# Gated mix of attention and a gated MLP on one core: GpSimd's batches planned with the wait for the maxima and with what ran over, and the exchange of token mixtures issued from ScalarE's queue

## The chip, the core and the metric

The kernel runs on one core of a Trainium2 chip, as one launch. The metric is the device time of that launch in microseconds (us). The engines are PE (matrix multiplications, with the loading of weights shown apart as PEld), DVE (VectorE), ACT (ScalarE), POOL (GpSimd) and SP (SyncE, which only issues transfers here); each has a queue of its own and takes its instructions in order. Sixteen DMA engines carry what the queues issue.

## What is computed

For 2048 tokens x of width 512 the result mixes an attention with 32 heads of width 16 and a gated MLP of inner width 1792, all in float32:

```python
g = _sigmoid((x * gate_w).sum(-1, keepdims=True))
a = _A_ref(x, A_wqkv, A_wo)      # softmax(q k^T / 4) v for 32 heads, then @ wo
b = _B_ref(x, B_w_gate, B_w_up, B_w_down)   # (sigmoid(x @ w_gate) * (x @ w_up)) @ w_down
return g * a + (1 - g) * b
```

## The kernel before

**Precision.** Products of the dense parts are made of three terms: each operand is split into a high part and a low remainder (`xh`, `xl` for the tokens; `...h`, `...l` for weights), and high*high, high*low and low*high are summed.

**The attention, step by step.** Heads go in pairs, 16 pairs, and a pair takes 16 steps `k`, 256 steps in all. A step holds, for a pair that comes later, 8 score products only for their row maxima (PE L288, each reduced by DVE at L290); 8 score products whose exponential ACT takes (PE L675, ACT L677); and the 16 products with the values (PE L825), whose sum ACT copies out (L830) and POOL adds up (L842). The maxima of half a pair are complete in one step of eight. DVE then transposes them (`mt`, L296), and `put_max` has POOL split them into two parts (`mhl`, L315 and L306); SP writes these to memory and reads them back as two further rows of `qs` (L308, L312), so that the second score product comes out with its maximum subtracted.

**The dense sums beside it.** PE also works off twelve half products (L162) a step from a generator, `filling`: q and k of other head groups ("qk"), then for the MLP's gate and up weights (and the last of q and k) the jobs "far" (steps 16 to 47, counted from 0), "side" and "chain" (steps 48 to 71 for q and k, 72 to 239 for gate and up), and the first heads. A job's sum is quartered, so that most sums take one step. Its result stands in one bank of PSUM (`dn`); ACT copies it out at the start of the next step (`leave`, L603), POOL combines it with earlier results (`plus`, L536), and SP stores it. The two halves of the PE array write the same bank, so the second half of a sum may begin only when the first is through. `turn` orders this with an empty instruction on POOL's queue, a **token** (L173): it waits for PE's first half, and PE's second half (L162) waits for it. As POOL takes its queue in order, a token is also behind all that was put on POOL ahead of it.

**What sets POOL's order.** POOL's work lies in lists: `later` (sums and maxima), `turnover` (weights of the next job), `slow` (mixtures of tokens) and `soon`. Each entry has a cost in us. `work(2.0)` right behind the token in the middle of a step and `work(2.6)` at its end take entries off the lists while more than 0.3 us of that length is left; `put_max` is put ahead of the rest at a step's end.

**The exchange of mixtures.** The jobs "side" and "chain" do not read the tokens themselves but differences of quarters of them, which were made by POOL during "far" and stored in `t_d`. `mixed_x(n, c, k0, cx)` brings mixture n into a quarter of `xh` and of `xl`: two transfers of 512 KB (L372). It is called 14 times: twice when "far" ends, four times each in the last "side" job of q and k, in its last "chain" job, and in the last "side" job of gate and up. `kept_x` stores what is overwritten.

**Queues.** All transfers go out on SP's queue. ACT, PE, DVE and POOL keep the order in which the program is written; SP's order is chosen by the scheduler. Each transfer counts its end on one of eight counters (named DMAHW in the order shown below), which the transfers take in turn, and a transfer waits, where it is issued, until the one before it on its counter has ended. The weights of the next job are loaded by SP (L108) into two buffers that POOL has to have read (`ca`, `cb`: the parts of a "chain" weight).

Of the kernel before, what the change touches and what calls it, by code (L numbers as in the profile page):

```python
# [12 lines left out]
F32 = mybir.dt.float32  # L13
# [33 lines left out]
def gated_mix(ctx, tc, x, xT, wqk, wv, wo, w_gate, w_up, w_down, gate_w, out):  # L47
    nc = tc.nc
    pe, act, dve, pool, sp = nc.tensor, nc.scalar, nc.vector, nc.gpsimd, nc.sync
# [26 lines left out]
    t_d = dram.tile([5, 2, 2, 2, P, 512], F32, name="t_d")  # L76
# [100 lines left out]

    later, turnover, slow, soon = [], [], [], []

    def work(length):  # L180
        while length > 0.3 and (later or turnover or slow):
            cost, step = (later or turnover or slow).pop(0)
            step()
            length -= cost

    def flush(queue):
        while queue:
            queue.pop(0)[1]()
# [23 lines left out]
    def unit(w, c):  # L212
        cols = slice(c * 512, (c + 1) * 512)
        return [(w[k], (xh[:, k, cols], xl[:, k, cols])) for k in range(KT)]
# [17 lines left out]
    def put_qk(r, dst, row, c):  # L232
        e = keep.tile([P, 2, 512], F32R, name=f"qe{row}_{c}", tag="ev", bufs=2)
        split_later(e[:, 0, :], e[:, 1, :], r, lambda: sp.dma_start(
            dst[:, row * P:(row + 1) * P, c * 512:(c + 1) * 512].rearrange("a p s -> p a s"), e.bitcast(F32)))
# [63 lines left out]
    def put_max(half):  # L299

        p, i = half
        mt = mrow.pop(half)
        hl = keep.tile([P, 2, 32], F32R, name=f"mhl{p}_{i}", tag="mhl", bufs=2)

        def low():
            pool.tensor_tensor(hl[:, 1, :], mt, hl[:, 0, :].bitcast(F32), ALU.subtract)  # L306
            d = max_d[2 * p + i]
            sp.dma_start(d.rearrange("k r a j -> (k r) a j"), hl.bitcast(F32))  # L308
            for b in (1, 0):
                for a in range(2):  # L310
                    r = 64 * b + 3 * DH + a
                    rows_in[p, i] = sp.dma_start(QS[p % 2][r:r + 1, i * 1024:(i + 1) * 1024].rearrange(  # L312
                        "o (t k j) -> o t k j", t=8, k=4).bitcast(F32),
                        d[:, 8 * b:8 * b + 8, a, :].rearrange("k t j -> t k j").unsqueeze(0))
        return [(0.2, lambda: pool.tensor_copy(hl[:, 0, :], mt)), (0.25, low)]  # L315


    wd = []
# [1 line left out]
    def quarter(w, k0, c):  # L320

        cols = slice(c * 512, (c + 1) * 512)
        return [((w[0][:, k, :], w[1][:, k, :]), (xh[:, k0 + k, cols], xl[:, k0 + k, cols])) for k in range(2)]
# [44 lines left out]
    def mixed_x(n, c, k0, cx):  # L368

        cols = slice(cx * 512, (cx + 1) * 512)  # L370
        for a, xs in enumerate((xh, xl)):
            sp.dma_start(xs[:, k0:k0 + 2, cols].bitcast(F32), t_d[n, a, c].rearrange("k p s -> p k s"))  # L372

    def o_and_r(u, ks, ot, rb):

# [8 lines left out]
    def filling():  # L384
        pairs = [(m, i) for i in range(HF) for m in range(2)]
        qk = [(2, 0), (3, 0)]
# [6 lines left out]
        def beside(m, i):  # L393
            return i + HF if m < 2 else i + 1
# [68 lines left out]
        def out_of(run, name):  # L463
            e = keep.tile([P, 512], F32, name=name, tag="er", bufs=6)
            leave(e, run.o)
            return e
# [5 lines left out]
        def sums_of(kind, n, ws):  # L472

            if kind == "qk":
                for c in range(NC):
                    for i, w in enumerate(ws):
                        run = Sum(bankd(), unit(w, c))
                        yield run
                        put_qk(out_of(run, f"qk{n}_{c}_{i}"), (q_d, k_d)[i], n, c)
            elif kind == "far":  # L480
                for m in range(2):
                    for c in range(2):
                        run = Sum(bankd(), quarter(ws[m], 2, c))
                        yield run
                        sp.dma_start(place(m, n, c) if n < HF else place(2 + m, 0, c), out_of(run, f"far{m}{n}_{c}"))
            elif kind == "side":
                m, i = n
                for c in range(2):
                    for a in range(2):
                        run = Sum(bankd(), quarter(ws[a], 2 * a, c + 2))  # L490
                        yield run
                        if n in (qk[-1], pairs[-1]):
                            mixed_x(1 + a, c, 2 * a, c + 2)
                        e = out_of(run, f"side{m}{i}_{c}{a}")
                        if a == 0:
                            first = e
                            sp.dma_start(place(m, beside(m, i), c + 2), e)
                        else:
                            plus(e, e, first, place(m, i, c + 2))
            elif kind == "heads":  # L500
                for u in range(EARLY):
                    while split_of[u] in later:
                        later.pop(0)[1]()
                    oh, ol = [t for t in first_heads(u)][:2]
                    for a in range(2):
                        cols = slice(a * P, (a + 1) * P)
                        run = Sum(bankd(), [((oh[:, k, cols], ol[:, k, cols]), ws[k]) for k in range(2)])
                        yield run
                        sp.dma_start(hp_d[2 * u + a], out_of(run, f"hp{u}_{a}"))
            else:  # L510
                m, i = n
                for c in range(2):
                    i2 = beside(m, i)
                    to = [place(m, i, c), place(m, i, c + 2), place(m, i2, c + 2), place(m, i2, c)]
                    for a, (k0, cx) in enumerate(((0, c), (2, c), (0, c + 2), (2, c + 2))):
                        if a in (0, 2):
                            part = keep.tile([P, 2, 512], F32, name=f"had{m}{i}_{c}{a}", tag="ev", bufs=2)
                        had = part[:, a % 2]
                        if a < 3:
                            sp.dma_start(had, to[a])  # L520
                        run = Sum(bankd(), quarter(ws[a], k0, cx))
                        yield run
                        if n == qk[-1] and a >= 2:
                            mixed_x(1 + a, c, 2 * a - 4, c + 2)
                        e = out_of(run, f"chain{m}{i}_{c}{a}")
                        if a in (1, 2):
                            plus(e, e, first)
                        if a < 3:
                            plus(had, e, had, to[a])
                        else:  # L530
                            plus(e, e, first, to[a])
                        first = e
# [31 lines left out]
        for job, nxt in zip(jobs, jobs[1:]):  # L564
            kind, n = job
            coming = None
            for at, run in enumerate(sums_of(kind, n, ws)):
                if kind == "far":
                    u, r = divmod(4 * n + at - 2, 6)
                    if r == 0 and u < 4:  # L570
                        flush(slow)
                        mix_load(u // 2, u % 2)
                    if r == 2 and u < 4:
                        mix_x(u // 2, u % 2)
                if job == ("chain", pairs[-1]):
                    if at == 4:
                        for u in range(4):
                            first_heads_load(u)
                    if at in (6, 7):
                        first_heads_split(at - 6)  # L580
                if kind == "heads" and at in (2, 4, 6):
                    if at == 2:
                        first_heads_load(4)
                    first_heads_split(at // 2 + 1)
                if at == ask[kind][0]:
                    coming = raws(*nxt)
                if at == ask[kind][1]:
                    new = weights(*nxt, coming)
                    end = turnover[-1]
                yield run  # L590
            while end in turnover:
                turnover.pop(0)[1]()
            ws = new
            if kind == "far" and n == HF:
                flush(slow)
                for c in range(2):
                    mixed_x(0, c, 2, c)
                for c in range(2):
                    kept_x(3, c, 0, c + 2)
                    kept_x(4, c, 2, c + 2)  # L600
# [254 lines left out]
    run = next(fill)  # L855
# [29 lines left out]
    for k in range(NPER):  # L885
        n = 2 * k
# [17 lines left out]
        if run and run.done():  # L904
            run = next(fill, None)
# [99 lines left out]
    for n, (c, f) in enumerate(chunks):  # L1005
# [4 lines left out]
        hl = ready[n]  # L1010
# [59 lines left out]
```

## Time and profile before

| | |
|---|---|
| time, median of 3 runs | 1698.55 us (1698.15 to 1700.3) |
| profiled execution: its own time, its span, granted clock | 1699.21 us, 1697.4 us, 0.999 |
| busy DVE, ACT, POOL | 1453.4 us (86%), 1365.5 us (80%), 938.1 us (55%) |
| bytes moved | 254.20 MB, DMA engines busy 48.4% of the span |

A span goes from the first to the last instruction of the profiled execution. Rows of the timeline give start, duration, engine, line of the kernel, operation and tiles; in brackets the idle time just before, and what ended it. SPq and POOLq are entries of the queues of SP and POOL. A busy PE is not a PE without loss, since a product that is held up by the one ahead of it can show as a longer one.

### The profile page before, as it was taken

Reading aid. Unit: us, or ns where it says so; the run is one execution under the profiler, and the core shown is the slowest. Engines: PE = TensorE matmul, PEld = TensorE weight load, DVE = VectorE, ACT = ScalarE, POOL = GpSimd, SP = SyncE. Lnnn points to the kernel's source line nnn. Section 1 sums busy time; section 2 is a strip of 40 time slices with the busy share of each in tenths; the row PEclk is TensorE's granted clock in tenths of the full one; section 3 lists DMA queues with packets and bytes.
Section 4 is the critical chain, followed back from the end, with each engine's and each line's share of the span. In section 5 each row is a group of like instructions: output and inputs, shape, how many; then the busy total and the mean of one; then the engine's idle time right before and its main releaser. Section 6 shows DMA issues by size and latency. Waiting matters only on the chain.

```text
span 1697.4 us, 34663 instructions
## 1 busy us (share of the span) xinstructions
PE 1686.8 (99%) x12485; PEld 1030.4 (61%) x12485; DVE 1453.4 (86%) x2347; ACT 1365.5 (80%) x2657; POOL 938.1 (55%) x920
## 2 busy tenths in 40 slices
PE   9999999999999999999999999999999999999999
PEld 7755555555555565555555555555555555558887
DVE  7988888888889998898788888888998888888753
ACT  4188898888888898888889898898988989984331
POOL 1034575546665666566576676766666667544010
PEclk9999999999999999999999999999999999999999
DMA  7512456365465455455635352524343434358862
GB/s 243 141 48 58 128 198 181 132 182 184 138 205 150 149 148 175 141 166 159 176 101 144 107 144 97 141 97 139 105 134 108 127 119 156 123 180 288 295 212 72
DMA packets 143756, 254.20 MB, mean 150 GB/s; under 512 B 24224, under 2 KB 36512, under 8 KB 140704
## 3 DMA queue, kind: packets, MB, share of 16 engines
q1 hardware_dynamic: 143584, 251.98, 48.4%
q8 instruction: 98, 1.61, 0.4%
q14 instruction: 74, 0.61, 0.1%
HBM read 149.42 MB, written 102.50 MB: 148 GB/s over the span
## 4 chain that ended last, share of the span: by engine, by line
PE 97%; DMA 1%; POOL 1%; issue 1%; DVE 0%; ACT 0%; SPq 0%; POOLq 0%; DVEq 0%
PE dn L162 29%; PE sm L825 27%; PE sm L288 12%; PE st L675 7%; PE sm L1015 5%; PE sm L675 5%; PE st L288 3%; PE st L162 2%; PE dn L1015 2%; PE st L1015 2%; PE st L639 1%; PE st L149 1%; PE sm L149 1%; DMA chain_7r<-in_w_up_dram 1%; DMA chain_3r<-in_wqk_dram 0%
## 5 line engine op out<-in xcount | busy, mean ns | idle before, releaser
L290 DVE TENSOR_REDUCE stat<-sm 128x1 f32<-128x512 f32 x1313 | 850.8, 685 | 152.4 <-PE sm L675 132.1
L677 ACT ACTIVATE p<-st 128x512 f32<-128x512 f32 x1019 | 617.8, 652 | 1.2 <-PE st L675 0.8
L677 ACT ACTIVATE p<-sm 128x512 f32<-128x512 f32 x1027 | 610.4, 631 | 5.9 <-PE st L675 4.9
L288 PE MATMUL sm<-ks,qs 48*128 48x512 f32 x1313 | 515.8, 435 | 0.1
L290 DVE TENSOR_REDUCE stat<-st 128x1 f32<-128x512 f32 x735 | 480.9, 682 | 0.1
L825 PE MATMUL sm<-p,v 128*17 128x512 f32 x4016 | 480.8, 596 | 0.0
L675 PE MATMUL sm<-qs,ks 64*128 64x512 f32 x1027 | 428.8, 420 | 0.0
L675 PE MATMUL st<-qs,ks 64*128 64x512 f32 x1019 | 426.4, 419 | 0.2 <-ACT p L677 0.2
L288 PEld LDWEIGHTS sm<-ks,qs 48*128 48x128 f32 x1313 | 234.1, 184 | 287.6 <-DVE stat L290 206.8
L842 POOL TENSOR_TENSOR sum<-sum,part 128x512 f32<-128x512 f32 x224 | 288.6, 1288 | 147.1 <-PE sm L675 136.6
L288 PE MATMUL st<-ks,qs 48*128 48x512 f32 x735 | 290.2, 395 | 0.0
L830 ACT ACTIVATE part<-sm 128x512 f32<-128x512 f32 x214 | 128.4, 600 | 128.8 <-issue 94.1
L825 PEld LDWEIGHTS sm<-p,v 128*17 128x17 f32 x4016 | 93.3, 97 | 227.3 <-issue 158.0
L536 POOL TENSOR_TENSOR chain<-chain,chain 128x512 f32<-128x512 f32 x96 | 124.1, 1292 | 166.8 <-PE sm L675 148.6
L675 PEld LDWEIGHTS st<-qs,ks 64*128 64x128 f32 x1019 | 187.7, 184 | 30.6 <-issue 3.4
L675 PEld LDWEIGHTS sm<-qs,ks 64*128 64x128 f32 x1027 | 189.4, 185 | 10.8 <-issue 5.1
L536 POOL TENSOR_TENSOR had<-chain,had 128x512 f32<-128x512 f32 x96 | 123.5, 1287 | 29.8 <-PE sm L675 14.8
L288 PEld LDWEIGHTS st<-ks,qs 48*128 48x128 f32 x735 | 137.2, 187 | 1.5 <-ACT v L658 0.3
L603 ACT ACTIVATE chain<-dn 128x512 f32<-128x512 f32 x128 | 88.7, 693 | 0.0
L536 POOL TENSOR_TENSOR side<-side,side 128x512 f32<-128x512 f32 x32 | 41.3, 1292 | 84.8 <-PE sm L675 69.8
L104 POOL TENSOR_TENSOR ol<-ot,oh 128x512 fp32r<-128x512 f32 (+1 forms) x8 | 14.5, 1810 | 98.4 <-ACT oh L101 98.4
L315 POOL CAST mhl<-mt 128x32 fp32r<-128x32 f32 x32 | 7.6, 238 | 102.7 <-DVE mt L296 102.7
(913 smaller groups left out, 3230.6 us busy)
## 6 DMA issues: line engine op xcount, KB each, us to landing
gul<-gu_d SPq DMA_DIRECT2D x56, 512.0 KB
had<-gu_d SPq DMA_DIRECT2D x84, 256.0 KB
gu_d<-had SPq DMA_DIRECT2D x84, 256.0 KB
gu_d<-side SPq DMA_DIRECT2D x56, 256.0 KB
pv_d<-sum SPq DMA_DIRECT2D x32, 256.0 KB
qs<-q_d SPq DMA_DIRECT2D x30, 256.0 KB
ks<-k_d SPq DMA_DIRECT2D x30, 256.0 KB
gu_d<-far SPq DMA_DIRECT2D x28, 256.0 KB
```

Of the source, the lines that this page charges most:

```text
L149: pe.matmul(o, a, b, start=(i == 0), stop=(i == len(ops) - 1))
L162: mm = pe.matmul(self.o, a[rows], b[rows], start=(self.n == 0), stop=(self.n == 2 * len(self.ops) - 1))
L288: pe.matmul(t, qs[r:r + KM, qt * P:(qt + 1) * P], ks[r:r + KM, g * 512:(g + 1) * 512], start=True, stop=True)
L290: dve.tensor_reduce(stat[half][:, b, qt % 8, g:g + 1], t, axis=AX.X, op=ALU.max)
L536: pool.tensor_tensor(to, u, w, ALU.add)
L603: leave = lambda e, o: act.activation(e, o, AF.Copy)
L675: pe.matmul(o, ks[r:r + KR, (kt + a) * P:(kt + a + 1) * P], qs[r:r + KR, q0:q0 + 512], start=True, stop=True)
L677: act.activation(pt[:, 2 * a + c, :], o, AF.Exp, scale=DH ** -0.5)
L825: pe.matmul(o[32 * c:32 * c + VW, :], v[:, 2 * k % 16 + a, h * VW:(h + 1) * VW], pts[c // 2][:, 2 * a + c % 2, :], start=(a == 0), stop=(a ...
L830: act.activation(e, o, AF.Copy)
L842: pool.tensor_tensor(s, s, e, ALU.add)
L1015: pe.matmul(down[t], a, b, start=(f == 0 and m == 0), stop=(f == NF - 2 and m == 5))
```

## The change

`work` charges each call with what the call before ran over its length. The cost of `put_max`'s first entry goes from 0.2 to 1.6 us. `mixed_x` issues from ACT's queue, and its calls move behind the copy of the sum (`out_of`) that ends the step's reading; the two calls for mixture 0 move from the end of "far" into the first "side" job.

```diff
@@ -177,11 +177,15 @@
     later, turnover, slow, soon = [], [], [], []
 
+    over = [0.0]
+
     def work(length):
+        length -= over[0]
         while length > 0.3 and (later or turnover or slow):
             cost, step = (later or turnover or slow).pop(0)
             step()
             length -= cost
+        over[0] = max(0.0, -length)
@@ -312,7 +316,7 @@
-        return [(0.2, lambda: pool.tensor_copy(hl[:, 0, :], mt)), (0.25, low)]
+        return [(1.6, lambda: pool.tensor_copy(hl[:, 0, :], mt)), (0.25, low)]
@@ -369,7 +373,7 @@
         cols = slice(cx * 512, (cx + 1) * 512)
         for a, xs in enumerate((xh, xl)):
-            sp.dma_start(xs[:, k0:k0 + 2, cols].bitcast(F32), t_d[n, a, c].rearrange("k p s -> p k s"))
+            act.dma_start(xs[:, k0:k0 + 2, cols].bitcast(F32), t_d[n, a, c].rearrange("k p s -> p k s"))
@@ -489,9 +493,11 @@
                         run = Sum(bankd(), quarter(ws[a], 2 * a, c + 2))
                         yield run
+                        e = out_of(run, f"side{m}{i}_{c}{a}")
+                        if n == qk[0] and c == 1:
+                            mixed_x(0, a, 2, a)
                         if n in (qk[-1], pairs[-1]):
                             mixed_x(1 + a, c, 2 * a, c + 2)
-                        e = out_of(run, f"side{m}{i}_{c}{a}")
@@ -520,9 +526,9 @@
                         run = Sum(bankd(), quarter(ws[a], k0, cx))
                         yield run
+                        e = out_of(run, f"chain{m}{i}_{c}{a}")
                         if n == qk[-1] and a >= 2:
                             mixed_x(1 + a, c, 2 * a - 4, c + 2)
-                        e = out_of(run, f"chain{m}{i}_{c}{a}")
@@ -593,8 +599,6 @@
             if kind == "far" and n == HF:
                 flush(slow)
-                for c in range(2):
-                    mixed_x(0, c, 2, c)
                 for c in range(2):
                     kept_x(3, c, 0, c + 2)
                     kept_x(4, c, 2, c + 2)
```

Lines of the changed kernel are four higher behind `work`, more behind `sums_of`. The order of PE is the same in both, instruction for instruction, apart from line numbers. Three places where it moves:

POOL, in "far", at the end of a step that completes maxima (`mhl`) and the beginning of the next. `far02`, `far12` are weights of the next job, `mix` and `mh` mixtures, `sum` the sums of values. Before:

```order
L842 TENSOR_TENSOR sum_0_2094<-sum_0_2094,part_2289 128x512
L339 TENSOR_TENSOR mix_00_2146<-mix_00_2147,mix_00_2146 128x512
L315 CAST mhl_1_2350<-mt_1_2337 128x32
L306 TENSOR_TENSOR mhl_1_2350<-mt_1_2337,mhl_1_2350 128x32
L139 CAST far02h<-far02r 128x256
L136 TENSOR_TENSOR far02l<-far02r,far02h 128x256
L139 CAST far12h<-far12r 128x256
L136 TENSOR_TENSOR far12l<-far12r,far12h 128x256
L842 TENSOR_TENSOR sum_0_2094<-sum_0_2094,part_2370 128x512
```

and now:

```order
L846 TENSOR_TENSOR sum_0_2094<-sum_0_2094,part_2289 128x512
L319 CAST mhl_1_2349<-mt_1_2336 128x32
L310 TENSOR_TENSOR mhl_1_2349<-mt_1_2336,mhl_1_2349 128x32
L139 CAST far02h<-far02r 128x256
L136 TENSOR_TENSOR far02l<-far02r,far02h 128x256
L846 TENSOR_TENSOR sum_0_2094<-sum_0_2094,part_2367 128x512
L139 CAST far12h<-far12r 128x256
L136 TENSOR_TENSOR far12l<-far12r,far12h 128x256
L343 TENSOR_TENSOR mix_00_2146<-mix_00_2147,mix_00_2146 128x512
L343 TENSOR_TENSOR mix_00_2147<-mix_00_2147,mix_00_2146 128x512
```

A `mix` operation ahead of the maxima and the pair of `far12` behind them go behind the next sum, that is behind the token of the next step's middle.

SP, where the last "side" job of q and k ends and the first "chain" job begins. `chain_2r`, `chain_3r` are raw weights of the second "chain" job, `side_..` results. Before:

```order
L538 DMA s_d<-side_01_4663 128x512
L372 DMA xh<-t_d 128x2x512
L372 DMA xl<-t_d 128x2x512
L497 DMA s_d<-side_10_4730 128x512
L372 DMA xh<-t_d 128x2x512
L372 DMA xl<-t_d 128x2x512
L108 DMA chain_2r<-in_wqk_dram 128x2x256
L108 DMA chain_3r<-in_wqk_dram 128x2x256
L538 DMA s_d<-side_11_4793 128x512
```

and now:

```order
L544 DMA s_d<-side_01_4658 128x512
L108 DMA chain_2r<-in_wqk_dram 128x2x256
L503 DMA s_d<-side_10_4725 128x512
L108 DMA chain_3r<-in_wqk_dram 128x2x256
L544 DMA s_d<-side_11_4791 128x512
```

The four transfers of mixtures are gone from this stretch, and `chain_2r` stands ahead of the store of `side_10`.

ACT, the last of the 14 calls, with what each row waits for in brackets (PE, DVE, Pool, Activation: counters of the engines):

```order
L681 ACTIVATE p_1_9730<-st_65 128x512 [waits PE_49]
L607 ACTIVATE side_11_9751<-dn 128x512 [waits DMAHW0_49,PE_49]
L376 DMA xh<-t_d 128x2x512 [waits DMAHW6_49]
L376 DMA xl<-t_d 128x2x512 [waits DMAHW7_49]
L834 ACTIVATE part_9769<-sm_69 128x512 [waits DVE_49,PE_49,Pool_49]
L681 ACTIVATE p_0_9781<-sm_71 128x512 [waits PE_49,Activation_49]
```

The two transfers stand between the copy of the dense sum and the copy of the values' sum, and each waits for a counter of the transfers.

## The prediction

> **What bounds the kernel now.** First the page: what is busy, and the chain that ended last.
>
> ```profile
> PE 1686.8 (99%) x12485; PEld 1030.4 (61%) x12485; DVE 1453.4 (86%) x2347; ACT 1365.5 (80%) x2657; POOL 938.1 (55%) x920
> PE 97%; DMA 1%; POOL 1%; issue 1%; DVE 0%; ACT 0%; SPq 0%; POOLq 0%; DVEq 0%
> ```
>
> PE bounds it; PE's order stays as it is, so the change can win only what PE loses between its products. To see that loss I read a table by stretches for the products with the values alone (L825, 16 in a step), so that the count gives the steps.
>
> ```profile
> core 0: us, PE busy (x) PEld busy (x), PEclk, DMA share, GB/s
> 90.47:405.37 314.90, 107.06 (x896) 20.73 (x896) 1.00 0.45 140
> 405.37:412.52 7.15, 1.92 (x17) 0.38 (x18) 1.00 0.53 196
> 412.52:812.08 399.56, 135.71 (x1136) 26.24 (x1136) 1.00 0.54 161
> 812.08:827.47 15.39, 4.57 (x32) 0.81 (x32) 0.89 0.82 192
> 827.47:995.04 167.57, 57.34 (x480) 11.09 (x480) 1.00 0.39 117
> 995.04:1173.72 178.68, 61.24 (x516) 11.91 (x520) 1.00 0.40 120
> ```
>
> The last stretch is 32 steps (516 counts four of the next): 178.68/32 = 5.584 us a step, the undisturbed pace. Against it the others have lost: 56 steps 314.90 - 312.70 = 2.2; one step (the 57th) 7.15 - 5.58 = 1.6; 71 steps 399.56 - 396.46 = 3.1; two steps 15.39 - 11.17 = 4.2; 30 steps 0.05. Together 11.1 us, and no more can be won in these steps. Next, PEld's waits in the windows 90 to 450, 450 to 812 and 812 to 1460, of each the row on the token:
>
> ```profile
> PEld dn L162 <- POOLq L173: 3.6, 5, 1.5
> ...
> PEld dn L162 <- POOLq L173: 1.4, 4, 0.5
> ...
> PEld dn L162 <- POOLq L173: 2.6, 1, 2.6
> ```
>
> The 3.6 us answer to the first two losses (3.8). Of the 3.1 the token explains 1.4; the rest is not at a token and stays. The 2.6 us wait lies in the two steps that lose 4.2; there the granted clock is 0.89 over the stretch, and the rest of the loss goes with that clock.
>
> **The plan of POOL.** The timeline of POOL at one of these losses, with PEld's row at its end:
>
> ```profile
> 204.76 0.21 POOL L315 CAST mhl<-mt 128x32 fp32r<-128x32 f32 x1 [1.81 <-DVE mt L296]
> 205.05 0.25 POOL L306 TENSOR_TENSOR mhl<-mt,mhl 128x32 fp32r<-128x32 f32 x1
> 205.25 0.40 POOL L139 CAST far02h<-far02r 128x256 fp32r<-128x256 f32 x1
> 205.72 0.73 POOL L136 TENSOR_TENSOR far02l<-far02r,far02h 128x256 fp32r<-128x256 f32 x1
> 206.40 0.40 POOL L139 CAST far12h<-far12r 128x256 fp32r<-128x256 f32 x1
> 206.88 0.74 POOL L136 TENSOR_TENSOR far12l<-far12r,far12h 128x256 fp32r<-128x256 f32 x1
> ...
> 206.91 0.18 PEld L162 LDWEIGHTS dn<-xh,far01h 64*128 64x128 f32 x1 [0.69 <-POOLq L173]
> ```
>
> POOL stands 1.81 us for the maxima, which the plan had at nothing, then does four operations; the token is through when the last of them has begun (206.88), and PE goes on at 206.91, 0.69 late. With 1.6 us charged, the new order puts only `far02` ahead of the token: it is through at 205.72, and PE, which wanted it at 206.91 - 0.69 = 206.22, does not wait. The margin is 0.5 us. The other places of this kind have the same two small operations last or fewer. The two operations that go behind the token take 0.48 + 0.70 us there; with the sum and the two mixtures that the new order puts beside them (three of the size of L842, 1.28 us below) the batch is 5.0 us, under the 5.58 of a step. So the token waits away from weights go to nothing: 3.6 - 1.5 = 2.1 in the first stretch, 1.4 in the second. What they cost if a later batch then runs over: the same again, so the bounds are 0 and 3.5; I take **3.5**.
>
> **The exchange off SP's queue.** At the 57th step the token is behind weights that have not landed. SP's queue, POOL and PEld there:
>
> ```profile
> 395.70 0.48 SPq L497 DMA_DIRECT2D s_d<-side  x1
> 399.92 0.36 SPq L372 DMA_DIRECT2D xh<-t_d  x1
> 400.33 0.46 SPq L372 DMA_DIRECT2D xl<-t_d  x1
> 400.85 0.46 SPq L108 DMA_DIRECT2D chain_2r<-in_wqk_dram  x1
> 401.36 1.52 SPq L108 DMA_DIRECT2D chain_3r<-in_wqk_dram  x1
> ...
> 392.78 1.30 POOL L536 TENSOR_TENSOR side<-side,side 128x512 f32<-128x512 f32 x1
> ...
> 405.03 1.29 POOL L842 TENSOR_TENSOR sum<-sum,part 128x512 f32<-128x512 f32 x1
> 409.28 0.73 POOL L444 TENSOR_TENSOR chain_2r<-chain_2r,chain_3r 128x256 f32<-128x256 f32 x1 [2.96 <-DMA chain_3r<-in_wqk_dram]
> ...
> 410.93 0.18 PEld L162 LDWEIGHTS dn<-xh,cb(2, 0)h 64*128 64x128 f32 x1 [1.53 <-POOLq L173]
> ```
>
> From 396.2 to 399.9 SP stands at a mixture that waits for PE, and the weights behind it go out 4 us after they could. Now the mixtures are gone from SP. But the new plan of POOL also puts `side` and a `sum` ahead of the last two operations on the buffer that `chain_3r` goes into: these ended when `side` began, 392.78, and now end at 392.78 + 2 x 1.25 + 0.69 + 1.29 = 397.3 (spacing of rows: `side` and `sum` 1.25; cast 0.69). `chain_3r` can go out at 397.3 in place of 401.36, 4.1 earlier, with the last mixture behind it rather than ahead. If it takes as long as now (401.36 to 409.28), it lands at 405.2, and POOL is free at 405.03 + 1.25 = 406.3: no wait, with 1.1 us in hand. The token follows the first L444 by 410.93 - 409.28 = 1.65, so at 407.95, and PE wants it at 410.93 - 1.53 = 409.4. Won: **1.5**. The same 400 us later:
>
> ```profile
> 806.64 0.36 SPq L372 DMA_DIRECT2D xh<-t_d  x1
> 807.63 0.51 SPq L108 DMA_DIRECT2D chain_0r<-in_w_up_dram  x1
> 808.19 0.44 SPq L108 DMA_DIRECT2D chain_7r<-in_w_up_dram  x1
> ...
> 799.51 1.29 POOL L536 TENSOR_TENSOR side<-side,side 128x512 f32<-128x512 f32 x1
> ...
> 812.03 1.28 POOL L842 TENSOR_TENSOR sum<-sum,part 128x512 f32<-128x512 f32 x1
> 817.11 0.72 POOL L444 TENSOR_TENSOR chain_0r<-chain_0r,chain_7r 128x256 f32<-128x256 f32 x1 [3.80 <-DMA chain_7r<-in_w_up_dram]
> ...
> 818.75 0.18 PEld L162 LDWEIGHTS dn<-xh,cb(0, 0)h 64*128 64x128 f32 x1 [2.63 <-POOLq L173]
> ```
>
> `chain_7r` can go out at 799.51 + 4.5 = 804.0 instead of 808.19, and lands 4.2 earlier, at 812.9; POOL is free at 813.3. That margin is only 0.4 us, but the token, 1.64 later at 814.9, has 1.2 more before PE wants it at 818.75 - 2.63 = 816.1. Won: the whole **4.2**, the clock's part with it. Bounds for both places: 0 (nothing lands sooner) and 5.8; I take 5.7.
>
> **What ACT pays.** ACT's rows around the last of the 14 places, and the rows of L372 taken together (min/median/max ns):
>
> ```profile
> 807.28 0.70 ACT L603 ACTIVATE side<-dn 128x512 f32<-128x512 f32 x1
> 808.54 0.60 ACT L830 ACTIVATE part<-sm 128x512 f32<-128x512 f32 x1 [0.57 <-issue]
> ...
> L372 SPq DMA_DIRECT2D xh<-t_d x14: 360/410/535, 350.9 to 806.6; - x14
> L372 SPq DMA_DIRECT2D xl<-t_d x14: 378/482/1104, 351.4 to 807.1; - x14
> ```
>
> A pair costs SP 0.41 + 0.48 = 0.89 us; on ACT no issue is on show. If the queue issues while L603 runs, 1.26 us (808.54 - 807.28) cover it and it costs nothing; if it waits for L603's end, 0.57 cover it and 0.32 are left, 14 times 4.5 us, since behind L830 ACT's exponentials follow without idle time. That SP's rows follow one another while their data are still under way speaks for the first; I take **0** and keep 4.5 for the range. No new wait for PE comes in: the copy ahead of the transfers has waited for the same sum. What is queued behind is L830 and eight exponentials a step, and PE waits for these.
>
> **Sum.** 3.5 + 1.5 + 4.2 = 9.2 us. The profiled execution took 1699.21; less 9.2 is 1690.0. It lies 0.66 above the median of the runs, 1698.55, so a median would be 1689.4. I say **1689.7 us**, 0.5% faster.
>
> **The rivals.** (1) *ACT pays*: 4.5 us of the gain go back, 1694.2. For it: ACT's exponentials have no idle time. Against: the copy of the values' sum has to wait anyway. (2) *The transfers bound the two places*: the DMA share is 0.82 in the stretch from 812, the bytes are the same, and 5.7 us stay: 1695.4. Against: at 395.7 to 399.9 no weight was even put out. The Trainium skill, page "DMA: Bandwidth & Descriptors", section "Issuing engines are not separate DMA queues", says that transfers from all queues run on the same 16 engines and that a second queue saves only the time of issuing; taken alone that is this rival and its 1695.4. The trace differs at this place, where what is saved is a wait of SP's queue and not its issuing. (3) *The plan only shifts POOL's lateness* to later tokens, 938.1 us of work being the same: 3.5 less, 1693.2. (4) *Slower: ACT stands at a counter.* Each transfer now waits on ACT until the transfer before it on its counter has landed; that can be a weight put out a few us before. `chain_7r` took 817.11 - 808.19 = 8.9 us. At four of the 14 places (the second and fifth call, and the last two) that neighbour was put out within the step before; were it put out 5 us earlier and took 8.9, ACT would stand 3.9, less 0.57 of idle 3.3. Four times that is 13 us, against 9.2 won: 1702.9. It decides from 9.2/4 + 0.57 = 2.9 us a place on. Against: the weights among these neighbours go out sooner than before, as worked out above.
>
> **Chances.** Forecast 0.56, rivals (1) 0.14, (2) 0.11, (3) 0.09, (4) 0.10. A measurement can tell about 0.2%, 3.4 us, from no change. Against the execution's 1699.2 the forecast gains 9.2, (3) 6.0, (1) 5.0 and (2) 3.8, which is only just over it: all of the first two, most of (1) and half of (2) make faster 0.80; the rest of these and a weak (4) make same 0.11; slower is 0.09. The lower end is all 11.1 us won, 1699.21 - 11.1 - 0.66 = 1687.4; the upper end takes in (1) to (3) with some to spare, 1697.0. What is left out is mostly (4).
>
> **What would show it.** Right: no PEld row on POOLq at L173 over 0.3 us between 90 and 1460; the step at 57 and the two from 129 at 5.6 us and the granted clock 1.00 there; SP's `chain_3r` and `chain_7r` out some 4 us earlier against the step; POOL without a wait at L444. ACT's rows of the transfers (L376) start within 0.3 us of the copy ahead of them, and L834 still 1.26 us behind it. Wrong: L834 later than that by 0.3 (1) or by several us behind a transfer (4); L444 still waiting (2); new rows on POOLq in the step behind the maxima (3).

## The result, and the profile after

| | before | changed |
|---|---|---|
| median | 1698.35 us (1697.88 to 1700.3, 4 runs) | 1689.48 us (1688.66 to 1691.14, 4 runs) |
| ratio, 95% interval | | 0.9947, 0.993 to 0.9964 |
| profiled execution: time, span | 1699.21, 1697.4 us | 1689.49, 1687.7 us |

The forecast was 1689.7 us; the changed kernel is 0.5% faster. On the page, the busy times and the head of the chain that ended last:

```profile
PE 1680.0 (100%) x12485; PEld 1026.4 (61%) x12485; DVE 1452.3 (86%) x2347; ACT 1362.8 (81%) x2657; POOL 936.6 (55%) x920
PE 97%; issue 1%; DVE 1%; POOL 0%; DMA 0%; ACT 0%; SPq 0%; POOLq 0%; DVEq 0%
```

DVE, ACT and POOL have the work that they had. PE's time is shorter because products that were held up were counted as long ones: in steps 129 and 130 some 90 products kept PE busy for 13.19 us before, and for 11.17 us now. The table by stretches of the prediction, for the products with the values (now L829) of the changed kernel, cut at the same steps:

```profile
core 0: us, PE busy (x) PEld busy (x), PEclk, DMA share, GB/s
90.60:403.20 312.60, 107.05 (x896) 20.72 (x896) 1.00 0.47 143
403.20:408.79 5.59, 1.91 (x16) 0.37 (x16) 1.00 0.38 145
408.79:806.45 397.66, 135.71 (x1136) 26.22 (x1136) 1.00 0.55 162
806.45:817.62 11.17, 3.82 (x32) 0.74 (x32) 1.00 0.98 212
817.62:985.07 167.45, 57.34 (x480) 11.07 (x480) 1.00 0.39 120
```

Row by row against before: 314.90 - 312.60 = 2.30; 7.15 - 5.59 = 1.56; 399.56 - 397.66 = 1.90; 15.39 - 11.17 = 4.22; 167.57 - 167.45 = 0.12. Together 10.1 us. The two executions differ by 9.7; the 0.4 between is in the stretches ahead of the first step and behind these. The two steps from 129 now run at 5.58 us with the clock at 1.00, while the transfers are busy for 0.98 of that time.

PEld's waits over the whole span of the changed kernel, the row on the token ahead of the second halves of the dense sums (9.7 us, 14 times, before):

```profile
PEld dn L162 <- POOLq L173: 2.2, 4, 0.6
```

All four lie ahead of 90 us, in the opening; between 90 and 1460 us the view has no row on POOLq any more.

**The plan.** POOL's timeline at the place of the prediction (204.76 to 206.91 before), and PEld's row of the same step:

```profile
204.84 0.21 POOL L319 CAST mhl<-mt 128x32 fp32r<-128x32 f32 x1 [3.03 <-DVE mt L300]
205.13 0.25 POOL L310 TENSOR_TENSOR mhl<-mt,mhl 128x32 fp32r<-128x32 f32 x1
205.33 0.40 POOL L139 CAST far02h<-far02r 128x256 fp32r<-128x256 f32 x1
205.80 0.73 POOL L136 TENSOR_TENSOR far02l<-far02r,far02h 128x256 fp32r<-128x256 f32 x1
206.50 1.28 POOL L846 TENSOR_TENSOR sum<-sum,part 128x512 f32<-128x512 f32 x1
...
206.04 0.18 PEld L162 LDWEIGHTS dn<-xh,far01h 64*128 64x128 f32 x1
```

POOL now stands longer for the maxima, 3.03 us against 1.81, because less was put ahead of them. It costs nothing: the token is through at 205.80, and PE's second half starts at 206.04 with no bracket behind it.

**The exchange.** At the 57th step (from 403.2), SP, POOL and PEld of the changed kernel:

```profile
392.16 0.39 SPq L108 DMA_DIRECT2D chain_2r<-in_wqk_dram  x1
...
394.90 0.38 SPq L108 DMA_DIRECT2D chain_3r<-in_wqk_dram  x1
...
404.10 0.74 POOL L448 TENSOR_TENSOR chain_2r<-chain_2r,chain_3r 128x256 f32<-128x256 f32 x1
...
407.05 0.18 PEld L162 LDWEIGHTS dn<-xh,cb(2, 0)h 64*128 64x128 f32 x1
...
795.32 0.43 SPq L108 DMA_DIRECT2D chain_0r<-in_w_up_dram  x1
...
798.11 0.64 SPq L108 DMA_DIRECT2D chain_7r<-in_w_up_dram  x1
...
807.36 0.74 POOL L448 TENSOR_TENSOR chain_0r<-chain_0r,chain_7r 128x256 f32<-128x256 f32 x1
```

`chain_3r` goes out 8.3 us ahead of the step's start (403.20 - 394.90), where it was 4.0 (405.37 - 401.36); `chain_7r` 8.3 (806.45 - 798.11), where it was 3.9 (812.08 - 808.19). L448, which had stood 2.96 and 3.80 us for them, has no wait.

**ACT.** Its timeline at one of the 14 places of the changed kernel (ACTq is its queue):

```profile
392.24 0.41 ACTq L376 DMA_DIRECT2D xh<-t_d  x1
392.31 0.69 ACT L681 ACTIVATE p<-st 128x512 f32<-128x512 f32 x1
392.69 0.51 ACTq L376 DMA_DIRECT2D xl<-t_d  x1
392.79 0.70 ACT L607 ACTIVATE side<-dn 128x512 f32<-128x512 f32 x1
394.08 0.60 ACT L834 ACTIVATE part<-sm 128x512 f32<-128x512 f32 x1 [0.59 <-PE sm L829]
```

Both transfers go out before the copy L607, which stands ahead of them in the program, has begun; the first even before the exponential ahead of that. L834 follows the copy after 1.29 us, as before, and waits for PE only.

### The profile page after: what moved, and what is told of

Its sections match the earlier page's. It is cut to its first block, busy times and chain, and to the rows that moved or that the text cites. A ratio compares the mean times of both kernels' runs of the same rounds, so it can differ in the third digit from the quotient of the medians.

```text
span 1687.7 us, 34644 instructions
## 1 busy us (share of the span) xinstructions
PE 1680.0 (100%) x12485; PEld 1026.4 (61%) x12485; DVE 1452.3 (86%) x2347; ACT 1362.8 (81%) x2657; POOL 936.6 (55%) x920
## 4 chain that ended last, share of the span: by engine, by line
PE 97%; issue 1%; DVE 1%; POOL 0%; DMA 0%; ACT 0%; SPq 0%; POOLq 0%; DVEq 0%
PE dn L162 30%; PE sm L829 27%; PE sm L292 13%; PE st L679 7%; PE sm L1019 5%; PE sm L679 4%; PE st L292 2%; PE dn L1019 2%; PE st L162 2%; PE st L1019 2%; PE st L643 1%; PE st L149 1%; PE sm L149 1%; PE st L829 0%; DVE stat L294 0%
## 5 line engine op out<-in xcount | busy, mean ns | idle before, releaser
L829 PE MATMUL sm<-p,v 128*17 128x512 f32 x4016 | 480.0, 595 | 0.0
L829 PEld LDWEIGHTS sm<-p,v 128*17 128x17 f32 x4016 | 93.1, 96 | 225.9 <-issue 155.1
L834 ACT ACTIVATE part<-sm 128x512 f32<-128x512 f32 x214 | 128.1, 599 | 126.5 <-issue 86.0
L607 ACT ACTIVATE chain<-dn 128x512 f32<-128x512 f32 x128 | 89.1, 696 | 0.0
```

The source lines that it names most:

```text
L607: leave = lambda e, o: act.activation(e, o, AF.Copy)
L829: pe.matmul(o[32 * c:32 * c + VW, :], v[:, 2 * k % 16 + a, h * VW:(h + 1) * VW], pts[c // 2][:, 2 * a + c % 2, :], start=(a == 0), stop=(a ...
L834: act.activation(e, o, AF.Copy)
```

## The experiments

Each kernel was timed against the kernel before on the same chip. Where steps are named, a step's length is the time from its first product with the values to that of the next step, read from the rows of that line; an undisturbed one is 5.58 us. The text counts steps from 1, as the prediction does; some expectations below count them from 0 (their 196 is the 197th).

| kernel | median (range), us | ratio to before, 95% interval |
|---|---|---|
| plan_only | 1696.04 (1691.18 to 1698.65) | 0.9978, 0.9968 to 0.9989 |
| exchange_only | 1693.89 (1692.93 to 1695.83) | 0.9971, 0.9958 to 0.9983 |
| on_sp | 1694.46 (1692.14 to 1696.62) | 0.9973, 0.9961 to 0.9985 |
| act_ahead | 1696.04 (1693.59 to 1697.87) | 0.9988, 0.9978 to 0.9997 |
| cost_only | 1689.42 (1689.03 to 1690.25) | 0.9945, 0.9932 to 0.9957 |
| carry_only | 1691.08 (1690.45 to 1691.3) | 0.9953, 0.9941 to 0.9966 |
| four_issues | 1705.32 (1703.32 to 1706.18) | 1.0036, 1.0024 to 1.0049 |
| dve_spread | 1691.04 (1690.52 to 1693.07) | 0.9955, 0.9942 to 0.9969 |
| first_early | 1691.39 (1691.1 to 1693.84) | 0.9957, 0.9944 to 0.9971 |
| dens_only | 1688.08 (1687.4 to 1690.07) | 0.9937, 0.9924 to 0.9949 |
| after_again | 1689.61 (1688.78 to 1689.72) | 0.9943, 0.993 to 0.9957 |
| cost_dens | 1689.16 (1688.07 to 1689.61) | 0.9941, 0.9929 to 0.9953 |

### One half of the change alone

plan_only is the kernel before with the two lines of the plan:

```diff
+    over = [0.0]
+        length -= over[0]
+        over[0] = max(0.0, -length)
-        return [(0.2, lambda: pool.tensor_copy(hl[:, 0, :], mt)), (0.25, low)]
+        return [(1.6, lambda: pool.tensor_copy(hl[:, 0, :], mt)), (0.25, low)]
```

> Only the plan of POOL (1.6 us for the maxima, and the charge for what ran over); the exchange stays on SP's queue at its old places. If the two parts add up, as the prediction has it, the token waits behind the maxima go (3.5 us) and those at the 57th and the 129th step stay (about 5.7 us of loss): 1694.9 us. If the plan only shifts POOL's lateness, or the later release of the weights' buffer delays the weights further, those two waits grow and the time is 1697 us or more. If the plan alone ends the two waits too, 1689 to 1690.

exchange_only is the kernel before with `mixed_x` on ACT's queue and its calls where the change has them:

```diff
-            sp.dma_start(xs[:, k0:k0 + 2, cols].bitcast(F32), t_d[n, a, c].rearrange("k p s -> p k s"))
+            act.dma_start(xs[:, k0:k0 + 2, cols].bitcast(F32), t_d[n, a, c].rearrange("k p s -> p k s"))
```

> Only the exchange: issued from ACT behind the copies, mixture 0 in the first side job; POOL's plan as before. If the parts add up: the waits at the 57th and 129th step go (5.7 us), the token waits behind the maxima stay (3.5 us): 1692.7 us. If the exchange needs the new plan to win, over 1695.

What PEld still waits for at tokens between 90 and 1460 us, first in plan_only:

```profile
PEld dn L162 <- POOLq L173: 3.6, 2, 3.1
```

then in exchange_only:

```profile
PEld dn L162 <- POOLq L173: 3.8, 9, 0.7
```

The halves part cleanly. With the plan alone the waits behind the maxima are gone and the two places of the exchange are left (two waits, the longest 3.1 us); with the exchange alone these two are gone and nine short ones behind the maxima are left. The medians are 2.4 and 4.6 us under the kernel before of their call (1698.49), 7.0 together, against 8.9 for both: the halves do not add. By the steps, the losses up to the 244th fall by 3.6 and 5.1 us, and by 10.1 with both. Of the 1.4 between, 0.6 is in plan_only at the exchange, where steps 129 and 130 take 9.99 and 7.08 us, 1.7 more than before, and step 57 takes 1.1 less; the rest is spread in exchange_only over single steps that lose 0.1 to 0.3 us, and why these come is not settled.

The two places of plan_only can be followed further. The weights go out as far ahead of the step as before (3.84 us at the 129th step, 3.89 before; 3.96 and 4.01 at the 57th), so a later release of their buffer is not it. What differs is when POOL can use them: 9.35 us behind the issue of `chain_7r`, where it was 8.92, and 6.76 behind that of `chain_3r`, where it was 7.92. At the 129th step the wait at the token grows from 2.63 to 3.12 us, and over the two steps the granted clock is 0.80 where it was 0.89. The ten runs of plan_only spread from 1691.18 to 1698.65 us, with a mean granted clock of 1.000 in the shortest and 0.997 in the longest; what these two waits cost differs from run to run, and the profiled execution is one of the long ones. That can be one reason why the medians do not add.

### The new places, but SP's queue

```diff
-            act.dma_start(xs[:, k0:k0 + 2, cols].bitcast(F32), t_d[n, a, c].rearrange("k p s -> p k s"))
+            sp.dma_start(xs[:, k0:k0 + 2, cols].bitcast(F32), t_d[n, a, c].rearrange("k p s -> p k s"))
```

> The changed kernel, but the mixtures are issued from SP's queue at the new places in the program (behind the copies, mixture 0 in the first side job). If what is won is SP's queue no longer standing at a mixture that waits for PE, the two waits at weights come back and the time is about 1695 us. If the moved places alone do it, 1689.5 us as changed.

SP and POOL of this kernel at the 57th step:

```profile
397.81 0.36 SPq L376 DMA_DIRECT2D xh<-t_d  x1
398.22 0.53 SPq L376 DMA_DIRECT2D xl<-t_d  x1
398.80 0.82 SPq L108 DMA_DIRECT2D chain_2r<-in_wqk_dram  x1
399.72 0.42 SPq L108 DMA_DIRECT2D chain_3r<-in_wqk_dram  x1
...
407.56 0.72 POOL L448 TENSOR_TENSOR chain_2r<-chain_2r,chain_3r 128x256 f32<-128x256 f32 x1 [3.37 <-DMA chain_3r<-in_wqk_dram]
```

and PEld's waits at tokens, 90 to 1460 us:

```profile
PEld dn L162 <- POOLq L173: 4.6, 2, 2.6
```

The weights again go out behind the last mixture, 4.8 us later than in the changed kernel (399.72 against 394.90), and POOL stands for them. By the medians the kernel is 5.0 us slower than the changed one. The bytes, the plan and the places are the same: the gain at these two steps is SP's queue being free. This tells against rival (2), and so does the share of 0.98 at full pace in the changed kernel. The rule of the Trainium skill, page "DMA: Bandwidth & Descriptors", section "Issuing engines are not separate DMA queues", that a second queue saves only the time of issuing, does not cover these 5.0 us: they are waits of the queue.

### Mixtures ahead of the copy

```diff
-                        e = out_of(run, f"side{m}{i}_{c}{a}")
                         if n == qk[0] and c == 1:
                             mixed_x(0, a, 2, a)
                         if n in (qk[-1], pairs[-1]):
                             mixed_x(1 + a, c, 2 * a, c + 2)
+                        e = out_of(run, f"side{m}{i}_{c}{a}")
```

and the same in "chain".

> The changed kernel, but the mixtures stand ahead of the copy of the dense sum on ACT's queue instead of behind it. ACT then waits for PE's sum at the transfer. If issuing runs ahead of ACT's arithmetic, as the changed kernel's profile shows it (a transfer's row begins before the copy does), the time stays at 1689.5 us within 1 us. If the issue time of about 0.9 us counts in front of the copy, the bank of the dense sum comes free later and 14 places cost 0.3 us or more each: 1694 us or more.

Neither came. Almost the whole loss is one step, the 128th, of 13.03 us. ACT's timeline there, with SP's row of the transfer that it names:

```profile
799.59 0.61 SPq L251 DMA_DIRECT2D qs<-q_d  x1
...
802.09 0.37 ACTq L376 DMA_DIRECT2D xh<-t_d  x1
802.21 0.68 ACT L681 ACTIVATE p<-st 128x512 f32<-128x512 f32 x1
808.05 0.37 ACTq L376 DMA_DIRECT2D xl<-t_d  x1
808.46 0.60 ACT L607 ACTIVATE side<-dn 128x512 f32<-128x512 f32 x1 [5.57 <-DMA qs<-q_d]
```

The second transfer shares a counter with a load of `qs` that SP put out at 799.59. ACT's queue stands until that has landed: its transfer goes out 8.5 us behind the load's issue, and the copy and the exponentials behind it stand with it. This is rival (4), at one place and at 5.57 us. By the counters in the two traces it is met because swapping the calls also shifts which transfer shares which counter: in the changed kernel the neighbour of the second transfer is an `xh` of ACT's own, out at 795.49, and the pair goes out at 801.08 and 801.48 without a stand. The first transfer of the pair has `chain_0r` as its neighbour in both kernels, out 5.7 to 5.8 us ahead of it and landed in time. Of that place apart, three steps (67, 68 and 72) lose 1.2 us in sum, and the other places nothing; that fits the first theory of the issues themselves. What the 1.2 us are was not tested.

### Twice the issues

```diff
-            act.dma_start(xs[:, k0:k0 + 2, cols].bitcast(F32), t_d[n, a, c].rearrange("k p s -> p k s"))
+            for k in range(2):
+                act.dma_start(xs[:, k0 + k, cols].bitcast(F32), t_d[n, a, c, k])
```

> The changed kernel with each mixture's two transfers cut in two, so that ScalarE's queue issues four at each of the 14 places, some 1.6 us in place of 0.9. Theory A (the queue issues them while the exponential ahead still runs, before the copy begins): at most 0.3 us later at a place and the sums' copies are waited for little, 1689.5 to 1692 us. Rival (the issues take ScalarE's time): 0.7 us more at each of 14 places, some 10 us, 1699 us. If ScalarE stands at a counter instead, it is one place with several us and a row of ScalarE's on a transfer.

Slower than before, but not by the rival's way. ACT's timeline at the first place, which loses, and at one that does not, with the copies L608 and L835 (L607 and L834 in the changed kernel):

```profile
370.18 0.70 ACT L608 ACTIVATE side<-dn 128x512 f32<-128x512 f32 x1
370.59 4.42 ACTq L377 DMA_DIRECT2D xl<-t_d  x2
375.13 0.60 ACT L835 ACTIVATE part<-sm 128x512 f32<-128x512 f32 x1 [4.26 <-DMA chain_2r<-in_wqk_dram]
...
387.65 0.70 ACT L608 ACTIVATE side<-dn 128x512 f32<-128x512 f32 x1
387.89 1.05 ACTq L377 DMA_DIRECT2D xl<-t_d  x2
389.07 0.60 ACT L835 ACTIVATE part<-sm 128x512 f32<-128x512 f32 x1 [0.73 <-PE sm L830]
```

At 387.65 four issues fit beside the exponentials; L835 comes 1.42 us behind the copy and waits for PE. At 370.18 the last of the four stands behind `chain_2r`, which SP had put out just before on the same counter, for 4.26 us. The lost time lies in three groups of steps only: 51 to 56 with 8.6 us, 67 to 74 with 2.3, 126 to 129 with 5.7, in sum 16.6, which is all by which this kernel's steps are longer than the changed kernel's. Of ACT's waits in the first group the trace puts 4.3 and 2.5 us down to transfers. In the last its third issue at the 14th place comes 2.5 us after the second (816.31 and 813.77), and it shares its counter with `chain_7r`, out at 808.65; but the row of L835 names another engine, so a stand at the counter is only inferred there. At steps 67 and 68, which lose 2.0 us, no row names a transfer either: L835 begins 0.12 us behind the end of the last issue (470.20 and 470.08, 476.97 and 476.85), and one of the four issues at 467.83 takes 1.23 us, so there it seems to be the issuing that costs. What is shown is that ScalarE pays several us for a stand, and nothing for four issues where they fit beside the exponential and the copy ahead of L835.

### The first mixture back in its old place, on ACT's queue

```diff
-                        if n == qk[0] and c == 1:
-                            mixed_x(0, a, 2, a)
@@
                 flush(slow)
+                for c in range(2):
+                    mixed_x(0, c, 2, c)
```

> The changed kernel with the first mixture's four transfers back at the end of the last far block, where the kernel before had them, but on ScalarE's queue. Theory (the queue runs ahead of the arithmetic, and where the data and the counters are free an issue costs nothing, so this part of the change was not needed): the steps there stay at 5.6 us, 1689.5 us. Rival (the place matters, since ScalarE stands behind writes that SP put out just before on the same counters, as it did with four issues): 2.5 to 5 us in one or two steps near 345 to 357 us, 1692 to 1695 us, and a row of ScalarE's on a transfer.

ACT's timeline at the place:

```profile
354.12 0.70 ACT L607 ACTIVATE far<-dn 128x512 f32<-128x512 f32 x1
354.29 1.63 ACTq L376 DMA_DIRECT2D xl<-t_d  x1
355.96 0.54 ACTq L376 DMA_DIRECT2D xh<-t_d  x1
356.54 0.55 ACTq L376 DMA_DIRECT2D xl<-t_d  x1
357.22 0.60 ACT L834 ACTIVATE part<-sm 128x512 f32<-128x512 f32 x1 [2.40 <-PE dn L162]
```

The rival's side in the time, with a smaller price, but not by its mechanism: L834 comes 3.10 us behind the copy and not 1.29, and step 48 takes 7.37 us, 1.8 too long, yet no row of ACT's names a transfer. The product that L834's row names is not what it needs: the products of its own sum were through at 355.29. It begins 0.13 us behind the end of the last issue (357.09), so the wait is put down to the issues. Four transfers in a row, one of which takes 1.63 us to issue, need 3.2 us (353.87 to 357.09); at the place shown for the changed kernel L834 comes 1.84 us behind the first issue, and that is all there is to cover them. So the move of this mixture, which the prediction had not priced, was needed once ACT issues it.

### The charge and the carry apart

cost_only takes the carry out of the changed kernel:

```diff
-    over = [0.0]
-        length -= over[0]
-        over[0] = max(0.0, -length)
```

> The changed kernel without the carry of what ran over; only the wait for the maxima is charged at 1.6 us. Theory A (the charge alone takes the operations out from ahead of the token; the carry does nothing for time): no POOLq row on a token over 0.3 us from 90 us on, 1689.5 to 1690.5 us. Theory B (both are needed, since a batch that ran over still comes late at the next token): token waits of 0.3 to 0.7 us come back at several of the steps behind the maxima, some 2 us in all, 1691.5 us.

carry_only has the carry and the old charge:

```diff
-        return [(1.6, lambda: pool.tensor_copy(hl[:, 0, :], mt)), (0.25, low)]
+        return [(0.2, lambda: pool.tensor_copy(hl[:, 0, :], mt)), (0.25, low)]
```

> The changed kernel with the old charge of 0.2 us for the maxima and only the carry. Theory A (the charge does it): the token waits of the kernel before stay, some 3.5 us above the changed kernel, 1693.0 us. Theory B (both share the work): the places where the batch before ran over are free, those where the batch is planned the same as before keep 0.4 to 0.5 us each, 1 to 2 us in all, 1691 us.

Between 90 and 1460 us cost_only has no row on a token; carry_only has this one:

```profile
PEld dn L162 <- POOLq L173: 2.3, 3, 1.0
```

Theory A for the charge: alone it gives the changed kernel's time, as far as the times can tell. The carry is not needed for the tokens, but not without use: beside the old charge it removes most of the nine waits that exchange_only keeps, and leaves three (steps 21, 29 and 37 at 6.39, 6.20 and 6.58 us), for 1.6 us in the median. Beside the new charge it may be worth a little too. Without it steps 97, 121, 158, 187 and 216 take 5.73 to 5.80 us in cost_only, and 5.72 to 5.79 in cost_dens below, which also lacks it; in both executions of the changed kernel they take 5.6. Step 102 is 0.18 us shorter without it. Over the 244 steps cost_only is 0.5 us longer than the changed kernel and 0.8 longer than its second execution. Why is not known.

### What is left: VectorE

The changed kernel's steps up to 244 still lose 2.3 us, in 78, 85, 102, 109, 197 and 205 for the most part. dve_spread moves VectorE's work in these:

```diff
-            if r in (3, 4):
-                logits(2 * t, r - 3)
+            if r in (3, 5):
+                logits(2 * t, r // 5)
-        if 192 <= k < 212:
+        if 192 <= k < 222 and k % 8 not in (4, 5):
```

> The changed kernel with VectorE's work spread: the second of a step's two logits two products later, and the first mixture's reciprocals kept out of the two steps in eight where the maxima are taken. Theory (what the changed kernel still loses in the steps to 244, 2.3 us, is VectorE's work coming together at steps 77, 84, 101, 108, 196 and 204): those steps go to 5.6 us, 1.5 to 2.3 us less, 1687.5 us. Rival (those losses are of the shared memory or of the queue and not of VectorE's load): the steps stay at 5.7 to 6.1, 1689.5 us.

dens_only has the last two of these lines alone.

> The changed kernel with only the first mixture's reciprocals kept out of the two steps in eight where the maxima are taken. Theory (the losses at steps 196 and 204, 0.6 us, are VectorE's work coming together there, and the logits are better left where they are): these two steps at 5.6 us, the rest as in the changed kernel, 1688.9 us; too little for the times to tell, so the steps decide. Rival (the reciprocals only move the loss): 0.1 to 0.5 us at other steps from 192 to 222, 1689.5 us.

In dve_spread the loss at 85 and 109 moves one step on and steps 104 and 116 now take 6.44 and 6.23; spreading the logits is no gain. The reciprocals (L787) are another matter. The windows of the changed kernel over steps 197 and 205 (by L829):

```profile
1185.98:1191.69 5.71, 1.91 (x16) 0.37 (x16) 1.00 0.18 64
...
1230.75:1236.81 6.06, 1.91 (x16) 0.37 (x16) 1.00 0.18 60
```

DVE's timeline in the second, where a reciprocal stands behind the transposed maxima:

```profile
1232.80 0.21 DVE L300 STREAM_TRANSPOSE mt<-mpad 128x32 f32<-128x32 f32 x1
1233.05 0.54 DVE L787 RECIPROCAL den<-den 32x64 f32<-32x64 f32 x1
```

The windows of dens_only over the same steps:

```profile
1185.00:1190.58 5.58, 1.91 (x16) 0.37 (x16) 1.00 0.18 64
...
1229.64:1235.23 5.59, 1.91 (x16) 0.37 (x16) 1.00 0.18 62
```

The 0.6 us are gone, and no other step from 192 to 222 has become longer. The last two runs ask whether the times show it: the changed kernel once more, and cost_only with dens_only's lines.

> The changed kernel once more, beside the shortest version on the same chip. Expected 1689.5 us if the 1.4 us between it and the version with the reciprocals moved are real; 1688 us if that difference was one of chips.

> The changed kernel without the carry and with the reciprocals kept out of the steps where the maxima are taken. Theory (the carry does nothing, the reciprocals cost 0.6 us at two steps): steps 196 and 204 at 5.6 us, no row on a token, 0.6 us or a little more under the changed kernel of the same call, about 1688.5 us. Rival (one of the two helps only beside the other): equal to the changed kernel of this call, or above it.

The changed kernel took 1689.61 us again, and not 1688. Steps 197 and 205 are at 5.58 and 5.57 in cost_dens, and it is 0.45 us under the changed kernel of its call, with ranges that overlap; over the 244 steps it is 0.4 us longer than that, since the steps that are longer without the carry outweigh the two. The two versions with the reciprocals moved lie 0.5 to 1.4 us under the changed kernel by their medians; the 0.6 us are shown by the steps, while the times cannot tell them from none. The rest of the 2.3 us changes with the execution: step 78 took 6.00 us in one execution of the changed kernel and 5.58 in the other.

## Why the prediction was right, step by step

- **The bound.** PE's steps, and what they lose against 5.584 us. Of the 11.1 us named as all there was to win, 10.1 were won.
- **Plan, 3.5 us taken.** Measured 2.30 + 1.90 = 4.2 by the windows, so the term was 0.7 too small. The first stretch was given 2.1 and gave 2.3; the second 1.4 and gave 1.9. The 1.7 us there that the prediction called lost to something else and staying did not stay whole: 1.2 is left, and part of that comes and goes between executions. The mechanism is shown by plan_only, exchange_only and cost_only. Of the change's two parts of the plan the charge alone is enough; the prediction's mechanism rested on the charge too, and it did not part the two.
- **57th step, 1.5, and steps 129 and 130, 4.2.** Measured 1.56 and 4.22. The weights go out 4.3 and 4.5 us earlier against the step, where 4.1 and 4.2 were worked out. The clock's part came with it: 0.89 there before, 1.00 now.
- **ACT pays 0.** Measured 0 at L834. The reason, that the queue issues while the copy runs, was right but too cautious: the first issue lies ahead of the copy's start by 0.55 us (392.24 against 392.79). The sign written down for it, within 0.3 us of the copy, was missed.
- **Rival (1)** fell for two issues a place, by L834 at 1.29 us and by four_issues at 387.65. It comes back where the issues are more or longer: 1.8 us in first_early and, as it seems, 2.0 us at steps 67 and 68 of four_issues. **Rival (2)** fell by on_sp. **Rival (3)** fell: no wait on a token is left in the steps.
- **Rival (4)** is real and was not met. Its mechanism shows in act_ahead and four_issues, with 5.57 and 4.26 us a place against the 3.3 worked out, and four_issues ends slower than before. Why the changed kernel is spared can be read from its counters. Twice a transfer of ACT's has as its neighbour a weight that was put out shortly before: `chain_2r` (369.83, ACT's transfer at 375.89) and `chain_0r` (795.32 and 801.08). They had 6.06 and 5.76 us to land, and that was enough, where the rival counted with 8.9; in four_issues ACT comes to `chain_2r` about 1.5 us behind its issue and can go on only 5.16 us behind it. The prediction's reason, that the weights go out sooner, holds for these two. Which transfers come to share a counter it could not foresee from that, and it shifts with the order of a few calls, as act_ahead shows.
- **The number.** The sum was 9.2 us; the medians differ by 8.9 and the two profiled executions by 9.7. The steps gave 10.1, most of the excess in the plan's term, and 0.4 was lost outside them. That the forecast lies within 0.2 us of the median is closer than its terms were, and in part luck.

## What to carry to other kernels

- Where a queue that issues transfers stands at one of them, look at what is queued behind it: the gain of another queue is that wait and not the issuing. Then look at whose counter each transfer shares, since a compute engine that issues can stand for a transfer of another queue, with all its arithmetic behind it.
- A planner's cost should hold the wait that the engine will stand through, and not only the operation: changing one number from 0.2 to 1.6 gave the same time, as far as the times can tell, as that number with the bookkeeping beside it.
- When two halves of a change are tried apart, let each be judged at its own steps; the medians need not add.

## What had not been expected of the hardware

- ACT's queue ran ahead of its arithmetic: transfers went out 0.55 us before an activation that stands ahead of them had begun (392.24 and 392.79), with the exponential before that not yet started.
- A stand of PE of two or three us cost more than itself here. With the wait of 2.63 us at steps 129 and 130 the granted clock was 0.89 over 15.39 us; without it 1.00. With 3.12 us in plan_only it was 0.80 over 17.08. At steps 57 and 58 a wait of 1.53 us, before, left it at 1.00 over 12.70 us, and one of 1.93 us, in on_sp, went with 0.88 over 14.75. The Trainium skill, page "TensorE: Matmul & The Clock Gate", section "HAM oscillation — how this bites in real kernels", names idle gaps over some 3.4 us as what brings the clock down; here it fell with a wait shown as 2.63 us, though the products around it were held up as well, so the two cannot be set against each other exactly.
